# A top-32 mask moved from VectorE to ScalarE and GpSimd in a fused attention and mixture-of-experts kernel

## The chip, the core and the metric

The kernel runs on one core of one Trainium2 chip. The metric is the device time of one execution in microseconds (us). The core's engines work side by side, each through its own queue in order, and wait for each other through semaphores: PE (TensorE: matmuls and transposes, with PEld for its weight loads), DVE (VectorE), ACT (ScalarE), POOL (GpSimd) and SP (SyncE, which here only issues DMAs). Line numbers (L270) are those of the kernel before.

## The reference, cut to what matters

```python
# q, k, v: (8, 8, 576, 64) float32; top_k = 32
scores = scale * np.matmul(q, k.transpose(0, 1, 3, 2))
kth = np.partition(scores, -top_k, axis=-1)[..., -top_k:-top_k + 1]
scores = np.where(scores >= kth, scores, -1000000000.0)
attn = np.exp(scores - np.max(scores, axis=-1, keepdims=True))
attn = attn / (np.sum(attn, axis=-1, keepdims=True) + 1e-09)
x = np.matmul(attn, v)               # rearranged to (4608, 512)
# mixture of experts, 8 experts, each token to the one with the largest logit
logits = x @ w_gate
...
h = np.maximum(x_sorted[lo:hi] @ w1[e], 0.0)   # w1[e]: 512 x 1024
y_sorted[lo:hi] = h @ w2[e]                    # w2[e]: 1024 x 512
```

Every row of scores keeps its 32 largest entries; the others get weight zero. The weighted values then go, token by token, through one of eight two-layer networks.

## The kernel before, in words

**Tiling.** There are 8 batches. A batch has 4 units, and a unit is a pair of heads, 576 x 576 scores each. The rows of a unit are cut into 9 tiles of 128 rows by 576 columns, and the tiles into 5 groups: four pairs (one tile of each head) and one single tile (the last 64 rows of both heads). A *step* is one group. A batch has 20 steps, the kernel 160 steps and 288 tiles.

**A step.** `scores` (L202) multiplies q by k on PE (L212) and ACT copies the result from PSUM to the tile `s` in SBUF (L217). `weights` (L220) does the top 32 on DVE. First the 576 columns are *folded*: `hl` holds the larger and the smaller of column j and column j + 288 (L233, L234, two-input instructions). On the larger half, four rounds of MAX8 (L241, the eight largest) and three of MATCH_REPLACE8 (L251, which strikes them out) give its 32 largest; one more MAX8 (L248) looks at the smaller half. From both lists come the threshold `thr` (L261, L265) and, on POOL, a small value `over` (L266) that tells at the end whether the fold could have missed something; then an exact version below L609 would run, which it doesn't here. While the rounds go on, ACT makes minus the row's maximum (`nbias`, L243) and the exponential of all 576 scores (`w`, L245). At the end of the step DVE multiplies `w` by the mask "score at least threshold" and sums the rows in the same instruction, with the sum read out after it (L270). `transposed` (L276) turns `w` around on PE (L284, L292), and ACT copies it out (L287, L289, L295, L297). After the single tile of a unit, `outputs` (L299) multiplies by v (L314), and transposes the result to px and pl (L318 to L323). Its inner function `scaled` (L328 to L351) divides by the row sums on DVE: L336 reads px.

**Batches and experts.** After a batch's last unit, `route` (L355) finds each token's expert, and five scatters on POOL (L395) write the tokens to rows in DRAM sorted by expert. Each full block of 128 tokens of one expert is then a block of work for `block` (L477): PE transposes (L481), two layers of matmuls (L491, L500), ACT between (L483, L496, L504, which makes `y`), and a scatter to the output on POOL (L505). Its inputs, 4 MB of weights among them, are loaded through SP (`load_block`, L462). A block is cut into 17 pieces, which the main loop hands out from the sixth step of a batch on (L594 to L596). Batches 2 to 7 have blocks to do beside attention; the blocks that come out of the last batch run alone, after all attention: this is the *tail*.

**What sets the order.** The main loop (L577) writes, for step i: the scores of step i + 1, the weights of step i, `settle` (the scaling of a finished unit, and `route`), `close` (transposes and outputs) of step i - 1, and pieces of expert blocks. A scheduler then puts each engine's queue in order: it follows the written order where it can and fills in later instructions where it expects a gap. The buffers of the pools bound how far it can run ahead: `s` and `hl` have 2, `w` has 3.

Of the kernel before, what the change touches and what calls it, by code (L numbers as in the profile page):

```python
# [9 lines left out]
F32 = mybir.dt.float32  # L10
I32 = mybir.dt.int32
AF = mybir.ActivationFunctionType
# [4 lines left out]

TOP_K = 32
NEG = -3.0e38
BIG = 3.0e38  # L20
EPS = 1e-9

# [19 lines left out]
def kernel(  # L42
# [139 lines left out]
    def load_unit(b, u):  # L182
        n = SimpleNamespace(u=u)
        qkb = k.load.tile([P, 2, S], F32, name="qkb")
        nc.sync.dma_start(qkb, qk[b, u, :, :, :])
        n.q, n.k = qkb[:, 0, :], qkb[:, 1, :]
        n.v = k.load.tile([P, KC, P], F32, name="vb")
        nc.sync.dma_start(n.v, v[b, u, :, :].rearrange("(c p) d -> p c d", p=P))
        return n
# [12 lines left out]
    def scores(n, tiles):  # L202
        todo = []
        got = []
        for i in tiles:
            ps = k.ps_s.tile([P, 2, SM], F32, name="sc")
            todo += [(ps, h, rows, cols) for h, rows, cols in parts(i)]
            got.append(ps)
        for j in range(2):
            for ps, h, rows, cols in todo:  # L210
                d = slice(h * D, (h + 1) * D)
                nc.tensor.matmul(  # L212
                    ps[rows, j, 0:HF], n.q[d, cols], n.k[d, j * HF:(j + 1) * HF], start=True, stop=True
                )
        s = k.att.tile([P, 2, 2, HF], F32, name="s")
        for m, ps in enumerate(got):
            nc.scalar.copy(s[:, m, :, :], ps[:, :, 0:HF])  # L217
        return s

    def weights(n, tiles, s):  # L220
        m_all = range(len(tiles))
        m2 = slice(0, len(tiles))
        tops = tops_of[k.top % NTOP]
        k.top += 1
        nbias = k.small.tile([P, 2], F32, name="nbias", bufs=3)
        w = k.att.tile([P, 2, S], F32, name="w", bufs=3)
        flat = [s[:, m, :, :].rearrange("p j k -> p (j k)") for m in m_all]
        if k.exact:
            src = list(flat)
            width = S  # L230
        else:
            hl = k.att.tile([P, 2, 2, HF], F32, name="hl")
            nc.vector.tensor_tensor(hl[:, 0, m2, :], s[:, m2, 0, :], s[:, m2, 1, :], op=ALU.max)  # L233
            nc.vector.tensor_tensor(hl[:, 1, m2, :], s[:, m2, 0, :], s[:, m2, 1, :], op=ALU.min)  # L234
            src = [hl[:, 0, m, :] for m in m_all]
            width = HF
        scr = k.att.tile([P, 2, width], F32, name="scr")
        R = TOP_K // 8
        for r in range(R):
            for m in m_all:  # L240
                nc.vector.max(out=tops[:, m, r * 8:(r + 1) * 8], in_=src[m])  # L241
            if r == 0:
                nc.scalar.mul(nbias[:, m2], tops[:, m2, 0], -scale)  # L243
                for m in m_all:
                    nc.scalar.activation(w[:, m, :], flat[m], AF.Exp, scale=scale, bias=nbias[:, m:m + 1])  # L245
                if not k.exact:
                    for m in m_all:
                        nc.vector.max(out=tops[:, m, TOP_K + 1:TOP_K + 9], in_=hl[:, 1, m, :])  # L248
            if r < R - 1:
                for m in m_all:  # L250
                    nc.vector.match_replace(  # L251
                        out=scr[:, m, :], in_to_replace=tops[:, m, r * 8:(r + 1) * 8],
                        in_values=src[m], imm_value=NEG,
                    )
                    src[m] = scr[:, m, :]
        c = 2 * tiles[0] if len(tiles) == 2 else 2 * NC
        if k.exact:
            thr = tops[:, :, TOP_K - 1]
        else:
            both = k.small.tile([P, 2, 9], F32, name="both")  # L260
            nc.vector.tensor_tensor(  # L261
                both[:, m2, :], _back(tops[:, m2, TOP_K - 9:TOP_K]), tops[:, m2, TOP_K:TOP_K + 9], op=ALU.min
            )
            thr = k.small.tile([P, 2], F32, name="thr", bufs=3)
            nc.vector.tensor_reduce(thr[:, m2], both[:, m2, :], axis=AX.X, op=ALU.max)  # L265
            nc.gpsimd.tensor_tensor(  # L266
                n.over[:, c:c + len(tiles)], tops[:, m2, TOP_K + 8], thr[:, m2], op=ALU.subtract
            )
        for m in m_all:
            nc.vector.scalar_tensor_tensor(  # L270
                out=w[:, m, :], in0=flat[m], scalar=thr[:, m:m + 1], in1=w[:, m, :],
                op0=ALU.is_ge, op1=ALU.mult, accum_out=n.z[:, c + m:c + m + 1],
            )
        return w

    def transposed(n, tiles, w):  # L276
        pair = len(tiles) == 2
# [236 lines left out]

    with ExitStack() as st:
        open_pools(st, False)
        unit_of = {(0, 0): load_unit(0, 0)}

        work = [(b, u, g) for b in range(B) for u in range(U) for g in groups]
        per_batch = U * len(groups)  # L520
# [23 lines left out]
        def close(last):  # L544
            nonlocal late
            b, u, g, w = last
            n = unit_of[b, u]
            transposed(n, g, w)
            if g == groups[-1]:
                late = (b, u, outputs(n))  # L550

        def settle():
            nonlocal late, left
# [18 lines left out]
                left += new * PIECES  # L572
                ahead()

        s_next = scores(unit_of[0, 0], groups[0])
        last = None
        for i, (b, u, g) in enumerate(work):  # L577
            n = unit_of[b, u]
            if g == groups[0]:
                open_unit(n)  # L580
                b2, u2 = (b, u + 1) if u + 1 < U else (b + 1, 0)
                if b2 < B:
                    unit_of[b2, u2] = load_unit(b2, u2)
            s_now = s_next
            if i + 1 < len(work):
                b2, u2, g2 = work[i + 1]
                s_next = scores(unit_of[b2, u2], g2)
            w = weights(n, g, s_now)
            settle()
            if last is not None:  # L590
                close(last)
            last = (b, u, g, w)
            at = i % per_batch
            if at >= FIRST:  # L594
                rest = left - (KEEP if b == B - 1 else 0)
                pieces(-(-rest // (per_batch - at)))  # L596
# [13 lines left out]
    with tc.If(again > 0):  # L610
        with ExitStack() as st:
# [7 lines left out]
            with tc.For_i(0, B, 1) as b:  # L619
                x = k.xp.tile([P, KC, XW], F32, name="x")  # L620
                nc.vector.tensor_copy(x[:, :, Dm + 1].bitcast(I32), ids)
                lg = k.small.tile([P, KC, E], F32, name="lg")
                for u in range(U):
                    n = load_unit(b, u)
                    open_unit(n)
                    for g in groups:
                        transposed(n, g, weights(n, g, scores(n, g)))
                    outputs(n)(x, lg)
                route(x, lg)
                nc.vector.tensor_scalar_add(ids, ids, S)  # L630
# [52 lines left out]
```

## Time and profile before

| | |
|---|---|
| median of 7 runs | 1796.81 us (1793.19 to 1799.84) |
| profiled execution | 1794.58 us, span 1792.9 us |
| mean granted clock of PE | 0.853 |
| busy: DVE, ACT, POOL | 1416.6, 721.3, 120.1 us |
| last threshold found | 1440.6 us |
| period of a unit on DVE, batches 0 and 1 | 43.3 us |

Times inside the span count from its start. A row of a group gives the line, the engine, the operation, the tiles it writes and reads, the shape and the count; then its busy time in us and the mean duration of one in ns; then how long the engine stood idle just before it and who ended that. A row of the timeline gives start and length in us, and in brackets the idle time before it with its releaser. Instructions on one engine can overlap at their ends, so the distance between two starts is what one takes from the engine's time. The granted clock is TensorE's, as a share of full speed.

The period of a unit and the time of the last threshold were read from the starts of L266, which runs once a step when the threshold is there: in batches 0 and 1 the five steps of a unit lie 8.6, 11.4, 8.5, 7.7 and 7.0 us apart.

### The profile page before, as it was taken

Reading aid. Unit: us, or ns where it says so; the run is one execution under the profiler, and the core shown is the slowest. Engines: PE = TensorE matmul, PEld = TensorE weight load, DVE = VectorE, ACT = ScalarE, POOL = GpSimd, SP = SyncE. Lnnn points to the kernel's source line nnn. Section 1 sums busy time; section 2 is a strip of 40 time slices with the busy share of each in tenths; the row PEclk is TensorE's granted clock in tenths of the full one; section 3 lists DMA queues with packets and bytes.
Section 4 is the critical chain, followed back from the end, with each engine's and each line's share of the span. In section 5 each row is a group of like instructions: output and inputs, shape, how many; then the busy total and the mean of one; then the engine's idle time right before and its main releaser. Section 6 shows DMA issues by size and latency. Waiting matters only on the chain. (4 is left out here: it accounts for less than half of the span.)

```text
span 1792.9 us, 24778 instructions
## 1 busy us (share of the span) xinstructions
PE 1537.1 (86%) x8126; PEld 982.7 (55%) x8126; DVE 1416.6 (79%) x4967; ACT 721.3 (40%) x1429; POOL 120.1 (7%) x268
## 2 busy tenths in 40 slices
PE   5777777879887999799979997999799938999996
PEld 3344444446444765476646654756466616666664
DVE  8999999999999999999999999999999930000000
ACT  3444444444444444454545553545454411111111
POOL 0000100010001000100010001000100010000000
PEclk9866666669866999699979996999799868999999
DMA  1000100034002640255326502653254138888883
GB/s 55 21 21 21 48 21 21 21 107 167 27 21 101 232 168 33 90 214 203 127 74 231 202 33 80 235 188 130 67 221 151 61 97 316 295 304 301 299 299 143
DMA packets 107561, 244.00 MB, mean 136 GB/s; under 512 B 5535, under 2 KB 26015, under 8 KB 107425
## 3 DMA queue, kind: packets, MB, share of 16 engines
q1 hardware_dynamic: 101040, 223.43, 34.6%
q0 software_dynamic: 6384, 18.92, 2.9%
q8 instruction: 66, 1.08, 0.2%
q14 instruction: 71, 0.57, 0.1%
HBM read 221.05 MB, written 23.11 MB: 136 GB/s over the span
## 5 line engine op out<-in xcount | busy, mean ns | idle before, releaser
L212 PE MATMUL sc<-qkb 64*128 64x288 f32 (+1 forms) x1280 | 377.4, 540 | 45.0 <-ACT s L217 38.5
L491 PE MATMUL ph<-xTs,w 128*128 128x128 f32 x2752 | 345.1, 283 | 28.6 <-ACT xTs L483 23.8
L241 DVE MAX8 tops<-scr 128x8 f32<-128x288 f32 x864 | 356.7, 448 | 1.2
L491 PEld LDWEIGHTS ph<-xTs,w 128*128 128x128 f32 x2752 | 327.9, 197 | 52.5 <-ACT xTs L483 34.4
L500 PE MATMUL py<-w,hT 128*128 128x512 f32 x688 | 316.9, 600 | 0.0
L284 PE MATMUL wTm<-ident,w 128*128 128x128 f32 x1152 | 218.7, 340 | 105.1 <-DVE w L270 83.6
L284 PEld LDWEIGHTS wTm<-ident,w 128*128 128x128 f32 x1152 | 168.1, 175 | 178.4 <-ACT nbias L243 44.5
L212 PEld LDWEIGHTS sc<-qkb 64*128 64x128 f32 (+1 forms) x1280 | 175.3, 217 | 163.5 <-ACT s L217 69.1
L251 DVE MATCH_REPLACE8 scr<-tops,scr 128x288 f32<-128x288 f32 x576 | 251.3, 443 | 0.0
L217 ACT COPY s<-sc 128x576 f32<-128x576 f32 x288 | 174.4, 641 | 181.0 <-DVE w L270 98.4
L270 DVE SCALAR_TENSOR_TENSOR w<-s,thr,w 128x576 f32<-128x576 f32 x288 | 224.1, 810 | 1.5 <-ACT w L245 0.3
L245 ACT ACTIVATE w<-s,nbias 128x576 f32<-128x576 f32 x288 | 212.4, 772 | 4.3
L500 PEld LDWEIGHTS py<-w,hT 128*128 128x128 f32 x688 | 124.0, 192 | 126.3 <-issue 126.0
L287 ACT COPY wT<-wTm 128x512 f32<-128x512 f32 x256 | 144.1, 590 | 97.9 <-PE wTm L284 97.1
L314 PE MATMUL po<-wT,vb 128*64 128x288 f32 x1024 | 154.9, 450 | 1.2 <-ACT wT L289 1.2
L496 ACT ACTIVATE hT<-ph 128x512 f32<-128x512 f32 x86 | 51.4, 598 | 206.4 <-PE ph L491 206.1
L241 DVE MAX8 tops<-hl 128x8 f32<-128x288 f32 x288 | 127.8, 451 | 0.0
L251 DVE MATCH_REPLACE8 scr<-tops,hl 128x288 f32<-128x288 f32 x288 | 125.9, 443 | 0.0
L233 DVE TENSOR_TENSOR hl<-s 128x576 f32<-128x576 f32 (+1 forms) x160 | 109.9, 687 | 19.7 <-ACT s L217 19.6
L248 DVE MAX8 tops<-hl 128x8 f32<-128x288 f32 x288 | 120.2, 446 | 0.0
L314 PEld LDWEIGHTS po<-wT,vb 128*64 128x64 f32 x1024 | 74.1, 150 | 80.0 <-issue 37.9
L234 DVE TENSOR_TENSOR hl<-s 128x576 f32<-128x576 f32 (+1 forms) x160 | 110.3, 690 | 0.0
(113 smaller groups left out, 938.9 us busy)
## 6 DMA issues: line engine op xcount, KB each, us to landing
w<-in_moe_w_dram SPq DMA_DIRECT2D x86, 2048.0 KB, 12.7
qkb<-in_qk_dram SPq DMA_DIRECT2D x32, 576.0 KB, 3.8
xg<-x_rows SPq DMA_DIRECT2D x43, 257.0 KB, 2.7
vb<-in_v_dram SPq DMA_DIRECT2D x32, 320.0 KB, 3.2
x_rows<-blank SPq DMA_DIRECT2D x9, 257.0 KB, 4.9
out_dram<-y,xg POOLq DMA_INDIRECT x43
x_rows<-x,posi POOLq DMA_INDIRECT x40
wg<-in_moe_w_gate_dram SPq DMA_DIRECT2D x1, 16.0 KB
```

The lines of the kernel that those rows point to most:

```text
L212: nc.tensor.matmul(ps[rows, j, 0:HF], n.q[d, cols], n.k[d, j * HF:(j + 1) * HF], start=True, stop=True)
L217: nc.scalar.copy(s[:, m, :, :], ps[:, :, 0:HF])
L241: nc.vector.max(out=tops[:, m, r * 8:(r + 1) * 8], in_=src[m])
L245: nc.scalar.activation(w[:, m, :], flat[m], AF.Exp, scale=scale, bias=nbias[:, m:m + 1])
L248: nc.vector.max(out=tops[:, m, TOP_K + 1:TOP_K + 9], in_=hl[:, 1, m, :])
L251: nc.vector.match_replace(out=scr[:, m, :], in_to_replace=tops[:, m, r * 8:(r + 1) * 8], in_values=src[m], imm_value=NEG,)
L270: nc.vector.scalar_tensor_tensor(out=w[:, m, :], in0=flat[m], scalar=thr[:, m:m + 1], in1=w[:, m, :], op0=ALU.is_ge, op1=ALU.mult, accum_o ...
L284: nc.tensor.transpose(pm[:, c * P:(c + 1) * P], w[:, m, c * P:(c + 1) * P], ident)
L287: nc.scalar.copy(n.wT[:, :, m, tiles[0] * P:(tiles[0] + 1) * P], pm4)
L314: nc.tensor.matmul(po[r, 0:HF], lhsT, rhs, start=(c == 0), stop=(c == KC - 1))
L491: nc.tensor.matmul(ph[:, f, :], n.w1[:, 0, dt, fc * P:(fc + 1) * P], xT[:, dt, :], start=(dt == 0), stop=(dt == DT - 1),)
L500: nc.tensor.matmul(py, hT[:, f, :], n.w2[:, 0, f, :], start=(f == 0), stop=(f == FT - 1))
```

## The change

`weights` is taken apart into four functions.

- `fold` makes `hl`. It is called for step i + 1 within the search of step i, ahead of its fourth round.
- `search` runs the rounds and makes `thr`. `nbias` is now made on POOL, and so is a new small value `low`, the threshold times 2^120.
- `depths` has ACT compute Relu(2^120 x (thr - s)) for each of the 288 tiles, into `w`: zero where the score is kept, a huge number elsewhere.
- The new `weights` subtracts it from the score on POOL (a two-input instruction over 128 x 576, one for each tile), and then ACT takes the exponential, now summing the rows itself. Masked entries become exp of a hugely negative number, zero.

The masked multiplication on DVE (L270) is gone. Exponential and Relu now both come after the threshold. `s` has three buffers where it had two; scores are written two steps ahead where it was one. The inputs of two units are loaded at the start, and a unit's inputs are asked for after the outputs of the unit two before it, where it was at the start of the unit before it. In the step, `settle` and `close` now stand between the search and `depths`.

```diff
-        s = k.att.tile([P, 2, 2, HF], F32, name="s")
+        s = k.att.tile([P, 2, 2, HF], F32, name="s", bufs=2 if k.exact else 3)
...
+    def fold(tiles, s):
+
+        m2 = slice(0, len(tiles))
+        hl = k.att.tile([P, 2, 2, HF], F32, name="hl")
+        nc.vector.tensor_tensor(hl[:, 0, m2, :], s[:, m2, 0, :], s[:, m2, 1, :], op=ALU.max)
+        nc.vector.tensor_tensor(hl[:, 1, m2, :], s[:, m2, 0, :], s[:, m2, 1, :], op=ALU.min)
+        return hl
...
         for r in range(R):
+            if r == R - 1:
+                between()
             for m in m_all:
                 nc.vector.max(out=tops[:, m, r * 8:(r + 1) * 8], in_=src[m])
             if r == 0:
-                nc.scalar.mul(nbias[:, m2], tops[:, m2, 0], -scale)
-                for m in m_all:
-                    nc.scalar.activation(w[:, m, :], flat[m], AF.Exp, scale=scale, bias=nbias[:, m:m + 1])
+                nc.gpsimd.tensor_scalar_mul(nbias[:, m2], tops[:, m2, 0], -scale)
...
+        low = k.small.tile([P, 2], F32, name="low", bufs=3)
+        nc.gpsimd.tensor_scalar_mul(low[:, m2], thr[:, m2], STEEP)
...
-        for m in m_all:
-            nc.vector.scalar_tensor_tensor(
-                out=w[:, m, :], in0=flat[m], scalar=thr[:, m:m + 1], in1=w[:, m, :],
-                op0=ALU.is_ge, op1=ALU.mult, accum_out=n.z[:, c + m:c + m + 1],
-            )
+        return low, nbias
+
+    def depths(tiles, s, low):
+
+        w = k.att.tile([P, 2, S], F32, name="w", bufs=3)
+        for m in range(len(tiles)):
+            nc.scalar.activation(
+                w[:, m, :], s[:, m, :, :].rearrange("p j k -> p (j k)"), AF.Relu,
+                scale=-STEEP, bias=low[:, m:m + 1],
+            )
         return w
+
+    def weights(n, tiles, s, w, nbias):
+
+        c = 2 * tiles[0] if len(tiles) == 2 else 2 * NC
+        for m in range(len(tiles)):
+            nc.gpsimd.tensor_tensor(
+                w[:, m, :], s[:, m, :, :].rearrange("p j k -> p (j k)"), w[:, m, :], op=ALU.subtract
+            )
+            nc.scalar.activation(
+                w[:, m, :], w[:, m, :], AF.Exp, scale=scale, bias=nbias[:, m:m + 1],
+                accum_out=n.z[:, c + m:c + m + 1],
+            )
...
-        unit_of = {(0, 0): load_unit(0, 0)}
+        unit_of = {(0, u): load_unit(0, u) for u in range(2)}
...
                 late = (b, u, outputs(n))
+                b2, u2 = divmod(b * U + u + 2, U)
+                if b2 < B:
+                    unit_of[b2, u2] = load_unit(b2, u2)
...
-            s_now = s_next
-            if i + 1 < len(work):
-                b2, u2, g2 = work[i + 1]
-                s_next = scores(unit_of[b2, u2], g2)
-            w = weights(n, g, s_now)
+
+            def between():
+                if i + 1 < len(work):
+                    hl_of[i + 1] = fold(work[i + 1][2], s_of[i + 1])
+
+            low, nbias = search(n, g, s_of[i], hl_of.pop(i), between)
             settle()
             if last is not None:
                 close(last)
+            w = depths(g, s_of[i], low)
+            if i + 2 < len(work):
+                s_of[i + 2] = ready(i + 2)
+            weights(n, g, s_of.pop(i), w, nbias)
             last = (b, u, g, w)
```

## The prediction, on record before the result

> **What bounds the kernel now.** I read the engine shares of the page, then the stages, then the order of instructions inside one group of rows.
>
> ```profile
> PE   1537.1 (86%) x8126; PEld 982.7 (55%) x8126; DVE 1416.6 (79%) x4967; ACT 721.3 (40%) x1429; POOL 120.1 (7%) x268
> ```
>
> Over the span PE looks busiest, but that is a mean over two unlike parts. The stages (columns: length, then busy time of PE, PEld, DVE, ACT, POOL with counts, granted clock, DMA share, GB/s) tell them apart:
>
> ```profile
> 60.00:190.00 130.00, 98.77 (x422) 53.79 (x420) 129.56 (x438) 58.40 (x117) 2.82 (x15) 0.69 0.07 22
> 414.00:546.00 132.00, 113.33 (x532) 67.31 (x532) 129.33 (x438) 61.42 (x122) 5.37 (x17) 0.78 0.12 42
> 594.00:726.00 132.00, 126.44 (x700) 81.69 (x700) 128.99 (x436) 64.95 (x130) 6.71 (x18) 0.91 0.32 114
> 774.00:908.00 134.00, 130.25 (x798) 85.71 (x796) 131.42 (x440) 68.67 (x135) 8.07 (x21) 0.99 0.42 149
> 956.00:1086.00 130.00, 122.89 (x702) 79.09 (x702) 129.27 (x437) 64.96 (x130) 7.29 (x19) 0.96 0.32 115
> 1134.00:1267.00 133.00, 127.71 (x786) 83.97 (x784) 130.48 (x436) 67.99 (x134) 7.69 (x19) 1.00 0.41 149
> 1315.00:1441.00 126.00, 120.47 (x674) 77.46 (x669) 120.86 (x410) 60.78 (x122) 7.40 (x19) 0.96 0.30 109
> 1485.00:1793.00 308.00, 280.68 (x1592) 202.46 (x1591) 0.00 (x0) 44.29 (x75) 18.70 (x19) 0.98 0.75 277
> ```
>
> These are the last fifteen steps of batches 0, 2, 3, 4, 5, 6 and 7, and the tail. Up to 1441 us DVE is busy without a break: it sets the pace. But PE, which does expert blocks beside attention from batch 2 on, comes close: in batches 4 and 6 it is 97% busy at a clock of 0.99 to 1.00, so it has nothing left there. The tail holds no attention; the change doesn't reach it. What DVE does:
>
> ```profile
> L270 DVE SCALAR_TENSOR_TENSOR w<-s,thr,w 128x576 f32<-128x576 f32 x288 | 224.1, 810 | 1.5 <-ACT w L245 0.3
> L245 ACT ACTIVATE w<-s,nbias 128x576 f32<-128x576 f32 x288 | 212.4, 772 | 4.3
> ```
>
> ```profile
> 18.71 0.80 DVE L270 SCALAR_TENSOR_TENSOR w<-s,thr,w 128x576 f32<-128x576 f32 x1
> 19.44 0.08 DVE L270 DVE_READ_ACCUMULATOR w<-s,thr,w 128x1 f32 x1
> 19.44 0.81 DVE L270 SCALAR_TENSOR_TENSOR w<-s,thr,w 128x576 f32<-128x576 f32 x1
> 20.18 0.08 DVE L270 DVE_READ_ACCUMULATOR w<-s,thr,w 128x1 f32 x1
> ```
>
> One lasts 0.81 us, but the next starts 0.735 us after it: that is what one takes from DVE's time.
>
> **The change, part by part.** *The mask leaves DVE:* 288 x 0.735 = 212 us, 36 x 0.735 = 26.5 us a batch. How much of it reaches the end is a matter of the stage. Batches 0 and 1 are DVE's alone (PE 98.8 of 130 at clock 0.69): 2 x 26.5 = 53. In the later six batches the first five steps (48 us, PE about 38.5) are DVE's too: 9 x 0.735 = 6.6 each, 40 in all. For their last fifteen steps (27 instructions, 19.8 us) I take as PE's floor its busy time times the clock, over 0.98: 113.3 x 0.78 / 0.98 = 90 for batch 2, so all 19.8 comes; 117 for batch 3 (132 - 117 = 15), 132 for batch 4 (2), 120 for batch 5 (10), 130 for batch 6 (3), 118 for batch 7 (8). Together 53 + 40 + 20 + 38 = **151 us**. When DVE's stall goes, PE is late next.
>
> *Relu on ACT:* 288 of the shape of L245, 0.77 us: 222 us, on an engine with 58 to 69 us of work in 130. Off the path as occupancy. The sum that moves from DVE to the exponential's accumulator may add an instruction on ACT; DVE's kind takes 0.08 us, so 0 to 23 us more, hidden in the same idle time. Relu, Exp and Copy already alternate behind one table load.
>
> *The subtraction on POOL:* 288 of 128x576 with two inputs. No row has that. Below: a memset of 128x513 at 517 ns, so 0.58 us. Above: the affine select of 128x128, 282 ns, as it stands is 2.2 ns an element, 1.27 us, doubled for two inputs 2.54. Taking off a fixed 129 ns (the 128x8 iota) leaves 1.2 ns an element: 0.8 us for one input, 1.5 for two; I take **1.5 us**, nearest to that row. So 288 x 1.5 = 432 us of about 1300, plus small ones (low, over, nbias at 0.19 us): no bound by occupancy.
>
> The Trainium skill (GPSIMD Engine Reference, Elementwise side by side) measured 4497 ns for a two-input add of 2048 elements; as an estimate that is 1.26 us for 576, and the sum would keep its size.
>
> *A longer way from threshold to weights.* Before, the masked weights stand 1.2 us after the threshold. Now: low 0.2, Relu 0.77, subtraction 1.5, exponential 0.77, some 0.3 for hand-overs: 3.5 us, 2.3 later. Most is covered, as PE takes the weights one step later. The cover is thin at one place, once a unit: DVE scales a unit's output (L336) after two more searches, and needs px from PE:
>
> ```profile
> 285.33 1.19 PE L323 MATMUL pl<-wg,oT 128*128 128x16 f32 x10
> ...
> 289.59 0.69 DVE L336 TENSOR_TENSOR x<-px,rz 128x512 f32<-128x512 f32 x1
> ```
>
> px ends at 285.39 here, so 4.2 us to spare. The change brings L336 forward by five masks (3.7 us) and px back by 2.3: 6.0 are needed. Over the 32 units the spare time is 3.7 to 5.1 us in batches 0 and 1, 4.4 to 7.8 in batch 2, mostly 5 to 8 later: new stalls of about 1.6 us in each of 8 units, 3 us in batch 2, 3 in first units later: **19 us**. Where PE is the floor the stall costs nothing more. Its bounds: 0 (PE's clock rises) to 2.5 times that with 2.54 us a subtraction.
>
> *Folds against subtractions.* The trace cannot show whether DVE's two-input folds (L233, L234, 0.67 us each) and POOL's reads get in each other's way; its POOL instructions are too small. Bounds: 0, and one subtraction a step (1.5 us x 160 = 240 us). The subtractions of a pair should end about 5 us after its threshold; the fold after next starts about 4.7 after it (a new step of 7.2 us, less 2.5): they just touch. I take 0.3 us a step where DVE is the pace, 85 steps: **26 us**.
>
> The Trainium skill (SBUF — State Buffer, Who interferes with whom) speaks against this change: a DVE instruction with two SBUF inputs and a GpSimd one that reads SBUF shut each other out, and whichever comes second waits to the end of the other. By it the term would grow towards its upper end if the two drift into step, and be 0 if folds always come first.
>
> *POOL's queue.* low, nbias and the subtraction stand behind the scatter L505, which waits for ACT's y:
>
> ```profile
> 796.10 1.01 POOL L505 DMA_INDIRECT out_dram<-y,xg  x1 [13.20 <-ACT y L504]
> 797.14 0.20 POOL L266 TENSOR_TENSOR over<-tops,thr 128x2 f32<-128x2 f32 x1
> ```
>
> The instruction behind it was ready at 794.0 and ran at 797.1. So far nobody waits for it; now ACT's Relu does, and behind that ACT's evacuations and PE. y, scatter and low are 0.69 + 1.01 + 0.2 = 1.9 us; for 24 blocks 0 to 46 us; I take 0.5 each, **12 us**. The five route scatters of a batch stand there too, where PE has time.
>
> *Folds and scores further ahead, and the load:* 0. The trace already has the next pair's fold (16.85) ahead of the present threshold (18.27), and a unit's inputs land in 3.8 us, a unit (43 us) before their use; with SP's longest wait, 37 us, that still holds. At worst a late load costs its landing, 8 x 3.8 = 30 us. A gain from a third s buffer is bounded by DVE's waits for s, 19.6 us. *At the end:* the last weights come 2.3 us later, in full: **2 us**.
>
> Sum: 151 - 19 - 26 - 12 - 2 = 92. The profiled execution took 1794.6 us (span 1792.9), so 1703; the median of the runs is 2.2 us above it: **1705 us**.
>
> **Rivals.** *A, full relief:* no losses, 1797 - 149 = 1648; with PE's floor softer than its busy share too, 1797 - 210 = 1587. For it: DVE idles under 1% in the first stage. Against: the spare time at L336. *B, slower:* POOL holds DVE. If one subtraction takes near 2.5 us, POOL is busy 5.6 of a step's 7.3 us, and each of the two folds meets one in flight and waits on average half of it: 2.5 us a pair against 1.47 gained, about 1.0 x 128 + 0.5 x 32 = 144 lost in place of the gain; minus what PE's floor hides (half), 1797 + 72 = **1870**. It decides from 1.47 us lost per pair, one whole subtraction. For it: only the bounds above. Against: the select's row gives 1.5. *C, moved, not removed:* ACT, held by Relus that wait for POOL, makes PE late wherever PE is the floor, and each step keeps its old pitch: 1755 to 1797, say 1780.
>
> **How the numbers follow.** Forecast (1650 to 1755) 0.58, A 0.13, B 0.20, C 0.09. The range 1630 to 1840 leaves out the lower part of A (0.05) and the upper of B (0.10); forecast and A alone would be 1587 to 1755. Faster by over 0.2%: 0.58 + 0.13 + 0.06 of C = 0.77; within 0.2%, about what this kernel's runs can tell from no change, 0.03; slower 0.20.
>
> **What would show it.** Right: in batches 0 and 1 a unit's period falls from 43.3 us to about 39, in batches 4 and 6 the fifteen steps stay near 131; DVE's idle time names px; POOL's subtraction reads near 1.5 us; L233 and L234 lengthen only now and then. Wrong: folds at 1.5 us and more (B), ACT's Relu waiting long for low while PE idles in batches 4 and 6 (C), or no idle time on DVE at all (A).

## The result and the profile after

The changed kernel took 1806.5 us (median; 1799.5 to 1813.7) beside 1797.0 us for the kernel before: ratio 1.0054, 95% interval 1.0044 to 1.0064. It is slower by half a per cent where 5% faster was forecast. Lines below are those of the changed kernel (L293); the profiled execution has a span of 1803.3 us.

What was to leave DVE did leave it. The page's engine shares, to be set beside those of before:

```profile
PE 1506.3 (84%) x8126; PEld 967.6 (54%) x8126; DVE 1283.2 (71%) x4391; ACT 915.2 (51%) x1845; POOL 624.7 (35%) x876
```

DVE is busy 133 us less, and POOL 505 us more. But the whole did not become shorter, so DVE must now stand idle. The stages say where (last fifteen steps of batches 0, 2, 4 and 6; columns as in the prediction):

```profile
55.00:176.00 121.00, 86.74 (x422) 49.36 (x420) 118.18 (x384) 76.27 (x156) 51.17 (x72) 0.74 0.08 23
389.50:512.00 122.50, 106.02 (x590) 65.70 (x589) 119.42 (x384) 81.50 (x169) 52.32 (x76) 0.89 0.15 52
737.70:881.00 143.30, 135.66 (x797) 88.71 (x794) 117.03 (x386) 84.86 (x170) 55.09 (x77) 0.98 0.38 137
1121.30:1269.80 148.50, 141.58 (x820) 92.99 (x821) 118.00 (x387) 86.05 (x173) 56.19 (x76) 0.96 0.37 132
```

Batches 0 and 2 got shorter (121 and 122.5 us, before 130 and 132) and DVE is still busy there nearly all the time: 118 us for 384 instructions, where 130 us less 27 masks of 0.735 us would be 110. Batches 4 and 6 got *longer* (143 and 148.5, before 134 and 133), and there DVE is idle for 26 and 30 us. PE is busy longer as well: 135.7 and 141.6 us, before 130.3 and 127.7; in batch 6 a part of that is more work in the stretch (820 instructions, before 786). So there are two kinds of loss: DVE needs more time for what it does, and DVE stands idle. The lengths of the batches, from the first threshold of one to the first of the next (the eighth to its last threshold), give the balance:

```
batch              0      1      2      3      4      5      6      7    then
before         171.6  175.7  179.9  180.5  181.5  178.1  181.5  173.3   352.4
after          157.0  167.4  168.3  178.5  190.6  191.8  197.2  173.3   360.2
difference     -14.6   -8.3  -11.6   -2.0   +9.1  +13.7  +15.7    0.0    +7.8
```

Thirty-six us are won by batch 3 and lost again by batch 6; the end adds 8. The last two columns belong together: of the 43 expert blocks (64 matmuls of the first layer each), 20 are now done after the last threshold, before 19, so batch 7 has one less. The tail, which the prediction held to be out of the change's reach, was reached in this way.

**First loss, on DVE itself.** The groups of the two folds before, then, after the change, of the subtraction, of the two folds, and of ACT's read-out of its accumulator:

```profile
L233 DVE TENSOR_TENSOR hl<-s 128x576 f32<-128x576 f32 (+1 forms) x160 | 109.9, 687 | 19.7 <-ACT s L217 19.6
L234 DVE TENSOR_TENSOR hl<-s 128x576 f32<-128x576 f32 (+1 forms) x160 | 110.3, 690 | 0.0
```

```profile
L293 POOL TENSOR_TENSOR w<-s,w 128x576 f32<-128x576 f32 x288 | 430.7, 1512 | 287.7 <-ACT w L283 286.1 <-DVE thr L269 0.7
L225 DVE TENSOR_TENSOR hl<-s 128x576 f32<-128x576 f32 (+1 forms) x160 | 133.4, 833 | 54.0 <-ACT s L218 53.0
L226 DVE TENSOR_TENSOR hl<-s 128x576 f32<-128x576 f32 (+1 forms) x160 | 125.9, 787 | 0.0
L296 ACT ACTIVATION_READ_ACCUMULATOR w<-w,nbias 128x1 f32 x288 | 54.4, 189 | 0.0
```

The folds took 687 and 690 ns in the mean before; now 833 and 787, together 39 us more. The 39 us lie on 43 of the 320 folds, some 0.9 us each, four to seven of them in every batch, and each of the 43 started while a subtraction was running. The timeline of batch 0 shows how one grows (start, length):

```profile
122.43 0.75 DVE L225 TENSOR_TENSOR hl<-s 128x576 f32<-128x576 f32 x1
123.35 3.28 POOL L293 TENSOR_TENSOR w<-s,w 128x576 f32<-128x576 f32 x2
123.47 1.90 DVE L226 TENSOR_TENSOR hl<-s 128x576 f32<-128x576 f32 x1
...
145.81 2.77 POOL L293 TENSOR_TENSOR w<-s,w 128x576 f32<-128x576 f32 x2 [1.65 <-ACT w L283]
146.36 0.91 DVE L373 TENSOR_TENSOR lg<-lg,lt 128x40 f32<-128x40 f32 x1
147.57 1.07 DVE L374 TENSOR_TENSOR lg<-lg,lt 128x40 f32<-128x40 f32 x1
```

The fold at 122.43 runs ahead of the subtractions and takes 0.75 us. Its twin starts 0.12 us after a subtraction has begun and takes 1.90. L373 and L374 add 40 elements to a row, 0.19 us each before; here they last 0.91 and 1.07 us, each ending with one of the two subtractions. So it is with the DVE instructions with two inputs in SBUF that meet a subtraction: folds +39.1 us, `both` (L265) +10.5, `doubt` (L355) +7.4, the sums of `lg` +13.2: **70 us**, where the prediction had 26. Others beside a subtraction don't show it: L361, which has one input in PSUM, took 693 ns in the seven cases that met one and 692 otherwise, and MAX8, which has one input, 445 and 444.

**Second loss, waiting for the weights.** One pair of tiles in batch 0, from the threshold to the transposes:

```profile
114.87 0.15 DVE L269 TENSOR_REDUCE thr<-both 128x2 f32<-128x18 f32 x1
115.54 1.44 ACT L283 ACTIVATE w<-s,low 128x576 f32<-128x576 f32 x2 [3.63 <-POOL low L271]
116.39 2.78 POOL L293 TENSOR_TENSOR w<-s,w 128x576 f32<-128x576 f32 x2 [0.73 <-ACT w L283]
117.83 0.78 ACT L296 ACTIVATE w<-w,nbias 128x576 f32<-128x576 f32 x1 [0.85 <-POOL w L293]
118.75 1.12 PE L309 MATMUL wTm<-ident,w 128*128 128x128 f32 x4 [6.30 <-ACT w L296]
119.20 0.78 ACT L296 ACTIVATE w<-w,nbias 128x576 f32<-128x576 f32 x1 [0.50 <-POOL w L293]
```

From 115.02 to 119.98 it is 5.0 us to the second tile, and that is one of the shortest: over the 128 pairs the median is 6.4 us and the mean 7.0 (before, the second mask was done 1.8 us after the threshold, the first 1.1). The prediction's 3.5 us is the time of the first tile alone. ACT stands still 0.85 and 0.50 us for POOL, and PE 6.3 us for ACT. In all PE stands idle 176.5 us before L309 for these exponentials; before, it was 83.6 us for the masks. What DVE waits for most is `px`; before, and after (the us in all, how many, the longest):

```profile
DVE x L336 <- PE px L318: 7.3, 1, 7.3
```

```profile
DVE x L361 <- PE px L343: 84.1, 29, 8.8
```

Of the 84.1, batch 0 and then batch 6 have:

```profile
DVE x L361 <- PE px L343: 1.4, 3, 0.5
```

```profile
DVE x L361 <- PE px L343: 16.8, 4, 5.8
```

So the wait stands where PE is near its floor, not in the batches where the prediction had put it. (Not all of it is a loss by the change: run 3 below has 54.7 us of it left.) One of batch 4 in the timeline:

```profile
787.13 0.78 ACT L296 ACTIVATE w<-w,nbias 128x576 f32<-128x576 f32 x1 [0.57 <-POOL w L293]
...
788.50 0.77 ACT L296 ACTIVATE w<-w,nbias 128x576 f32<-128x576 f32 x1 [0.49 <-POOL w L293]
789.27 0.38 ACT L340 COPY oT<-po 128x288 f32<-128x288 f32 x1
...
790.39 2.15 PE L348 MATMUL pl<-wg,oT 128*128 128x16 f32 x10
790.43 0.69 DVE L361 TENSOR_TENSOR x<-px,rz 128x512 f32<-128x512 f32 x1 [6.00 <-PE px L343]
```

PE had finished its second product at 787.4, but ACT copied it out only at 789.27: two exponentials that wait for POOL stood ahead of that copy in ACT's queue. That is 1.85 us of the 6.00 that DVE waits here. PE idles, and afterwards is slow (ten small matmuls in 2.15 us; 1.19 in the prediction's line of before). Over the whole of batches 4, 5 and 6 PE's idle time grew from 13, 16 and 14 us to 24, 25 and 23, and its busy time went from 168, 162 and 167 to 166, 167 and 174: the larger part is idle time.

After the gap of 6.30 us above, L309's four transposes took 1.12 us, and 0.66 us where the gap was 0.49. The page TensorE: Matmul & The Clock Gate of the Trainium skill (Why this matters for your kernels) says that idle gaps of more than about 3 us put the array back to half its clock. The trace agrees as far as it goes: after each of the 14 gaps of over 5 us the four took 1.11 or 1.12 us. But after 18 gaps of 1 to 2 us they took 1.11 in the median too, so the gap just before does not decide alone.

### The profile page after: what moved, and what is told of

Same layout as the page of the kernel before. It is cut to its first block, busy times and chain, and to the rows that moved or that the text cites. A ratio compares the mean times of both kernels' runs of the same rounds, so it can differ in the third digit from the quotient of the medians.

```text
span 1803.3 us, 25580 instructions
## 1 busy us (share of the span) xinstructions
PE 1506.3 (84%) x8126; PEld 967.6 (54%) x8126; DVE 1283.2 (71%) x4391; ACT 915.2 (51%) x1845; POOL 624.7 (35%) x876
## 5 line engine op out<-in xcount | busy, mean ns | idle before, releaser
L293 POOL TENSOR_TENSOR w<-s,w 128x576 f32<-128x576 f32 x288 | 430.7, 1512 | 287.7 <-ACT w L283 286.1
L309 PE MATMUL wTm<-ident,w 128*128 128x128 f32 x1152 | 212.0, 326 | 181.2 <-ACT w L296 176.5
L213 PE MATMUL sc<-qkb 64*128 64x288 f32 (+1 forms) x1280 | 344.2, 528 | 17.6 <-ACT s L218 10.7
L296 ACT ACTIVATE w<-w,nbias 128x576 f32<-128x576 f32 x288 | 223.4, 776 | 181.7 <-POOL w L293 180.6
L309 PEld LDWEIGHTS wTm<-ident,w 128*128 128x128 f32 x1152 | 156.4, 166 | 258.2 <-ACT w L296 227.0
L283 ACT ACTIVATE w<-s,low 128x576 f32<-128x576 f32 x288 | 212.8, 774 | 119.1 <-POOL low L271 111.3
L213 PEld LDWEIGHTS sc<-qkb 64*128 64x128 f32 (+1 forms) x1280 | 166.7, 215 | 114.1 <-issue 43.7
L225 DVE TENSOR_TENSOR hl<-s 128x576 f32<-128x576 f32 (+1 forms) x160 | 133.4, 833 | 54.0 <-ACT s L218 53.0
L530 POOL DMA_INDIRECT out_dram<-y,xg x43 | 43.6, 1014 | 335.8 <-ACT y L529 330.8
L250 POOL TENSOR_SCALAR nbias<-tops 128x2 f32<-128x2 f32 (+1 forms) x160 | 35.1, 220 | 306.5 <-DVE thr L269 180.2
L226 DVE TENSOR_TENSOR hl<-s 128x576 f32<-128x576 f32 (+1 forms) x160 | 125.9, 787 | 0.0
```

What stands on the lines that cost most here:

```text
L213: nc.tensor.matmul(ps[rows, j, 0:HF], n.q[d, cols], n.k[d, j * HF:(j + 1) * HF], start=True, stop=True)
L283: nc.scalar.activation(w[:, m, :], s[:, m, :, :].rearrange("p j k -> p (j k)"), AF.Relu, scale=-STEEP, bias=low[:, m:m + 1],)
L293: nc.gpsimd.tensor_tensor(w[:, m, :], s[:, m, :, :].rearrange("p j k -> p (j k)"), w[:, m, :], op=ALU.subtract)
L296: nc.scalar.activation(w[:, m, :], w[:, m, :], AF.Exp, scale=scale, bias=nbias[:, m:m + 1], accum_out=n.z[:, c + m:c + m + 1],)
L309: nc.tensor.transpose(pm[:, c * P:(c + 1) * P], w[:, m, c * P:(c + 1) * P], ident)
```

## The experiments

Two theories, and a rival to both. *Port*: DVE's two-input instructions and POOL's reads shut each other out, which costs some 70 us. *Late weights*: the longer way from the threshold makes `px`, and PE, late. *Rival*: the new order (scores and folds ahead, loads later) is what costs. Each run was timed beside the kernel before; differences between runs are those of the ratios, times 1797 us. In runs 1 to 3 the weights have other values, so the result is not that of the reference, but the work is the same: PE has 8126 matmuls in each.

**1. POOL writes but does not read.** The subtraction is replaced by two memsets per tile that take as long together; for that the tiles `w` are 796 wide. (Each experiment's profile has its own line numbers, a few off.)

```diff
-            nc.gpsimd.tensor_tensor(
-                w[:, m, :], s[:, m, :, :].rearrange("p j k -> p (j k)"), w[:, m, :], op=ALU.subtract
-            )
+            for _ in range(2):
+                nc.gpsimd.memset(w[:, m, :], 0.0)
```

> The subtraction is replaced by two POOL memsets of 796 elements (about 0.7 us each by the 513-element row, together near the 1.41 us of the subtraction): POOL only writes, and the way from threshold to weights keeps its length. The weights are then a constant instead of the masked exponential. Theory 'late weights' (the way from threshold to weights grew from 1.6 to 5 us, so DVE waits for px and PE waits for weights and cools): the folds go back to 220 us of busy time (they are 259 in the changed kernel), DVE's wait for px stays near 80 us, the time is about 1765 us. Theory 'port' (the subtraction and DVE's two-input instructions shut each other out, 70 us of DVE time): 1730 us or less. Theory 'order' (the new written order alone costs the time): about 1800 us.

1738.4 us, ratio 0.9665 (0.9638 to 0.9693): 70 us less than the changed kernel, between the two ranges and nearer to that of *port*. The groups:

```profile
L295 POOL MEMSET w<- 128x796 f32 x576 | 418.0, 762 | 321.1 <-ACT w L284 317.8
L226 DVE TENSOR_TENSOR hl<-s 128x576 f32<-128x576 f32 (+1 forms) x160 | 110.0, 687 | 49.1 <-ACT s L219 49.0
L227 DVE TENSOR_TENSOR hl<-s 128x576 f32<-128x576 f32 (+1 forms) x160 | 109.9, 687 | 0.0
```

POOL is as busy as before (418 us), in the same places, and the folds are back at 687 ns. POOL's subtraction, which reads SBUF, holds DVE; a memset, which only writes, doesn't. The way to the weights is as long as it was (median 6.6 us), and the wait for `px` grew to 108 us: part of the time that DVE gets back it spends there. That the time fell by the same 70 us by which the instructions had been longer is chance, since the waits changed too.

The Trainium skill says this in SBUF — State Buffer, under Who interferes with whom: a DVE instruction with two SBUF inputs contends with a GpSimd instruction that reads SBUF, not with one that only writes it. These two runs agree on both halves, with 833 and 687 ns.

**2. Weights early, POOL still reads.** The exponential runs during the search, unmasked, and feeds PE; Relu and subtraction still run after the threshold, into a tile `d` that nobody reads.

```diff
+                w = k.att.tile([P, 2, S], F32, name="w", bufs=3)
+                for m in m_all:
+                    nc.scalar.activation(
+                        w[:, m, :], s[:, m, :, :].rearrange("p j k -> p (j k)"), AF.Exp, scale=scale,
+                        bias=nbias[:, m:m + 1], accum_out=n.z[:, c + m:c + m + 1],
+                    )
...
-            w = depths(g, s_of[i], low)
+            d = depths(g, s_of[i], low)
...
-            weights(n, g, s_of.pop(i), w, nbias)
+            weights(n, g, s_of.pop(i), d, None)
```

> The exponential is taken from the unmasked scores as soon as the row maximum is known, and PE gets that; Relu and subtraction still run, 288 each, into a tile that nobody reads. The mask is left out of the result. Late weights: DVE's wait for px (84 us) and PE's for weights vanish, POOL's subtractions still lengthen the folds: 1670 to 1700 us. Port: folds and small two-input instructions keep some 70 us of extra time and the kernel stays above 1780. Order: stays at 1800.

1758.5 us, ratio 0.9777 (0.9751 to 0.9804): 50 us less than the changed kernel, above the 1670 to 1700 of *late weights* and below the 1780 of *port*. Folds still 133.8 and 123.7 us. PE's wait before the transposes falls from 176.5 to 60.7 us, but DVE's wait for `px` only from 84.1 to 52.7; it was expected to vanish. So neither theory is the whole loss.

**3. Both at once:** run 2 with the memsets of run 1 in place of the subtraction.

> Both together: early unmasked weights, and memsets for the subtractions. Late weights and port as the two causes: the full relief, 1630 to 1660 us, PE being the limit in batches 3 to 7. Order: 1780 or more.

1663.4 us, ratio 0.9248 (0.9223 to 0.9273), 3 us above the expected range: 145 us less than the changed kernel, where the two alone give 70 and 50. Each loss hides part of the other: DVE that is held by POOL would otherwise wait for `px`, and the other way round. A unit takes 36.3 us in batches 0 and 1 (43.3 before). This is what the change would bring without either loss. The same batch lengths as above, from the profiles, say where each run gives time back against the changed kernel (us):

```
                      batches 0 to 2   3 to 7   then
run 1 (no reading)              15.5     54.0   -1.7
run 2 (weights early)            3.9     33.6    9.4
run 3 (both)                    47.6     86.9    7.1
```

Neither loss belongs to one stage. Even the port costs most where PE is near its floor. And in batches 0 to 2 late weights cost little only as long as the port hides them: in run 1 DVE waits 31 us for `px` there (7 in the changed kernel), and batch 0 gains next to nothing (156.6 us, 157.0). What DVE waits in batches 3 to 7 is not all loss either. Its idle time there is 142 us in the changed kernel and still 95 in run 3, with this wait for `px`:

```profile
DVE x L365 <- PE px L347: 54.7, 13, 8.1
```

There PE, busy 91 to 95% of each of these batches, is near its floor, and DVE waits for it.

**4. The order alone.** The order of the changed kernel, the mask on DVE as before, the exponential early.

```diff
+        for m in m_all:
+            nc.vector.scalar_tensor_tensor(
+                out=w[:, m, :], in0=s[:, m, :, :].rearrange("p j k -> p (j k)"), scalar=thr[:, m:m + 1],
+                in1=w[:, m, :], op0=ALU.is_ge, op1=ALU.mult, accum_out=n.z[:, c + m:c + m + 1],
+            )
-        return low, nbias
+        return w
...
-            w = depths(g, s_of[i], low)
...
-            weights(n, g, s_of.pop(i), w, nbias)
```

> The changed kernel's order (folds one step ahead, scores two ahead, three s buffers, loads after the outputs), but the mask back on DVE with the early exponential, and nbias on ACT. Late weights or port: within 1% of the kernel before, 1785 to 1805 us. Order: 1806 us or more, and the wait for px or the slow second step of batches 5 and 7 (26 us) appear here too.

1785.0 us, ratio 0.9931 (0.9905 to 0.9958). The rival falls: with the mask on DVE the order brings 12 us, it costs none. Its batches: 170.5, 175.0, 180.3, 177.7, 181.7, 176.3, 181.9, 167.2 us. From here the balance of the whole change reads: order -12, mask off DVE -123 (run 3 against run 4), its two losses +145, sum +10.

**5. Folds ahead of the first round, scores three steps ahead.** The folds should be done before the subtractions begin.

```diff
-            if r == R - 1:
+            if r == 0:
                 between()
...
-            if i + 2 < len(work):
-                s_of[i + 2] = ready(i + 2)
+            if i + 3 < len(work):
+                s_of[i + 3] = ready(i + 3)
...
-        s = k.att.tile([P, 2, 2, HF], F32, name="s", bufs=2 if k.exact else 3)
+        s = k.att.tile([P, 2, 2, HF], F32, name="s", bufs=2 if k.exact else 4)
```

> The changed kernel with one thing moved: the fold of the next step is called ahead of the first round of a search, not the fourth, and scores are written three steps ahead (four s buffers), so that DVE's folds run around the threshold, before POOL's subtractions of that step begin about 1.2 us after it. The work is the same. Port theory (the loss is in folds that meet subtractions in flight): folds back to 0.69 to 0.75 us each, 45 to 65 us less DVE time, and as in the run without POOL's reads the wait for px then grows to about 105 us, so 1740 to 1765 us. Rival (a subtraction costs DVE its time wherever the folds stand, or the time is only that of the late weights): folds stay at 0.8 us, 1790 to 1810 us.

1778.5 us, ratio 0.9897 (0.9864 to 0.9931), between the two ranges. The folds fell to 123.9 and 121.3 us, 25 us above before in place of 39: the place matters, but 40 of the folds still meet a subtraction, now mostly that of one step earlier. Two things were changed, so run 11 takes them apart.

**6. The new mask only where DVE sets the pace,** in batches 0 to 2; from batch 3 on the mask on DVE. `own` names the tiles that are masked on DVE; they have the early exponential, the others go the new way.

```diff
+            own = range(len(g)) if b >= 3 else ()
-            low, nbias = search(n, g, s_of[i], hl_of.pop(i), between)
+            low, nbias, w = search(n, g, s_of[i], hl_of.pop(i), between, own)
```

> The order of the changed kernel everywhere; the mask by Relu, POOL and late exponential only in batches 0, 1 and 2, the mask on DVE with the early exponential from batch 3 on. Theory (the gain is real where DVE alone is the pace, and late weights cost where PE is near its floor): batches 0 to 2 as in the changed kernel (157, 167, 168 us), batches 3 to 7 as in the run with only the order (177 to 182): 1785 less 13, 8 and 8 gives 1750 to 1765 us. Rival (what is won early comes back as waiting for expert blocks or at the end): 1780 to 1800 us.

1756.2 us, ratio 0.9764 (0.9726 to 0.9803), inside the expected range. Batches 0 to 2 take 157.1, 166.0 and 174.9 us (batch 2 is 6.6 us longer than in the changed kernel), the others 176.9, 181.7, 176.2, 181.7 and 166.7, as in run 4. What is won early stays won; against the mask on DVE the new mask gains in batches 0 to 2 and loses in batches 3 to 7.

**7. One tile of each pair.** The first tile of a pair on DVE, the second by POOL (144 of 288).

```diff
+            own = (0,) if len(g) == 2 or u % 2 else ()
```

> The changed kernel, but of each pair of tiles the first is masked on DVE with the early exponential, and only the second by Relu, POOL's subtraction and the late exponential (single tiles alternate): 144 of 288 tiles each way. Theory (lock and late weights both grow with the number of tiles in the chain): half of DVE's 212 us leave, the folds' lock halves to 25 to 40 us, the way from threshold to weights is some 3.5 us instead of 5.0 and the wait for px falls below 40 us: 1735 to 1775 us. Rival (one subtraction a step is enough for the lock, and one late tile for the late weights): 1785 to 1815 us.

1806.8 us, ratio 1.0050 (1.0029 to 1.0071). The time is in the rival's range, 32 us above the theory's. Batches 0 to 2 keep 24 of the 34 us that the changed kernel wins there, but batches 3 to 7 take 924 us, the changed kernel's 931, run 4's 885. The wait for `px` did fall below 40 us, as the theory had it, and that for `s` from 53.0 to 37.2. But DVE is busy 70 us more than in the changed kernel, and it has a new wait, for ACT's early exponentials:

```profile
DVE hl L225 <- ACT s L218: 37.2, 24, 5.4
DVE x L379 <- PE px L361: 33.9, 13, 10.8
DVE w L288 <- ACT w L256: 19.6, 9, 3.6
```

**8. `low` and `nbias` on DVE,** out of POOL's queue.

```diff
-                nc.gpsimd.tensor_scalar_mul(nbias[:, m2], tops[:, m2, 0], -scale)
+                nc.vector.tensor_scalar_mul(nbias[:, m2], tops[:, m2, 0], -scale)
...
-        nc.gpsimd.tensor_scalar_mul(low[:, m2], thr[:, m2], STEEP)
+        nc.vector.tensor_scalar_mul(low[:, m2], thr[:, m2], STEEP)
```

> The changed kernel with low and nbias made on DVE, not on POOL; the subtraction stays on POOL. If the queue on POOL (low and nbias behind scatters and subtractions) were what makes the weights late: 1780 us or less. If it is a small term, as the few waits of ACT for low say (the change's 320 small instructions cost DVE 20 to 30 us where it is the pace): 1795 to 1820 us.

1825.7 us, ratio 1.0181 (1.0130 to 1.0232), a little above the range: the 320 small instructions last 85 us on DVE (359 and 173 ns each), DVE is busy 52 us more in all, and the wait for `px` fell only from 84 to 76 us. So moving the small instructions doesn't pay. It does not settle POOL's queue, since the subtraction still stands in it: in the pairs its wait after its Relu grew from 10.6 to 35.5 us. In the changed kernel `low` starts more than 0.3 us after its threshold in 23 of the 160 steps, 57.5 us in all, 33 of them behind the five route scatters, once in each of seven batches. What that costs is open.

**9. As 6, and the single tile that ends a unit on DVE in batches 0 to 2.**

```diff
+            own = range(len(g)) if b >= 3 or len(g) == 1 else ()
```

> The mixed kernel (Relu, POOL and late exponential only in batches 0 to 2), and there the single tile that ends each unit goes back to DVE with the early exponential: 96 of 288 tiles by POOL. Theory (in the stages that DVE paces, what is left of the late weights is the wait for px, and px hangs on the unit's last tile): the second step of a unit in batches 0 to 2 falls from 12.2 us to about 10 for 0.74 us more in another step, 12 units by about 1.5 us: 1735 to 1750 us. Rival (px waits as long on the pair ahead of the single tile): 1755 to 1770 us.

1756.6 us, ratio 0.9764 (0.9734 to 0.9795): no gain, and in the rival's range. The second step of a unit fell by about 1 us, less than expected, the single tile's own step grew by 0.8 (6.5 to 7.3 us), and the step after it by up to 1.3.

**10. The single tile on DVE in all batches** of the changed kernel.

```diff
+            own = (0,) if len(g) == 1 else ()
```

> The changed kernel with only the single tile that ends each unit masked on DVE with the early exponential, in all batches: 256 of 288 tiles by POOL. If px waits because the unit's last tile is late: the wait for px falls from 84 us to under 40, against 32 x 0.74 = 24 us more DVE work: 1765 to 1795 us. If px waits because PE is behind with the pairs too, above all from batch 3 on: the wait stays over 60 us and the time 1800 to 1825 us.

1770.3 us, ratio 0.9843 (0.9805 to 0.9881), 38 us less than the changed kernel. The waits for `px` fell from 29 to 14, but those that are left are long (58.0 us in all): the time is in the first range, the wait between the two. The gain is in batches 4 to 7 (187.1, 182.9, 185.8 and 158.2 us), none of it in batches 0 to 3.

**11. Scores three steps ahead, folds where they were** (the second half of the diff of run 5).

> The changed kernel with the scores three steps ahead and four s buffers, the fold left ahead of the fourth round. It takes apart the run in which both were changed (1778 us). If that gain came from the place of the folds: 1798 to 1815 us here. If it came from the scores being there earlier: 1770 to 1785 us, and the folds keep their 0.8 us.

1755.5 us, ratio 0.9760 (0.9722 to 0.9797): 53 us less than the changed kernel, with every mask still on POOL, and 15 us below even the lower range. So the gain of run 5 did not come from the folds' place. Here they keep 129.5 and 131.6 us, and run 5, which moves them too, is 25 us slower than this one, for a reason that I didn't pin down. DVE's waits in this run:

```profile
DVE x L361 <- PE px L343: 70.3, 30, 9.2
DVE hl L225 <- ACT s L218: 26.6, 18, 5.5
```

The wait for `s` halves (53.0 us in the changed kernel). All of the gain lies in batches 3 to 7: 172.2, 184.0, 176.6, 182.5 and 162.4 us; batches 0 to 2 are 5 us longer.

**12 to 14. What the third step of lead is.** Run 12 is the control: run 4 with the same lead. Run 13 has the fourth buffer and the old lead. Run 14 joins 10 and 11.

> Control for the run with scores three steps ahead: the same fourth s buffer and the same three steps in the kernel that has only the order (mask on DVE, early exponential; 1785 us with two steps ahead). Theory (the missing lead is a need that the new mask makes, since the scores stay in use until POOL has subtracted and ACT and PE meet them late): 1780 to 1788 us, no gain to speak of, for DVE waits only 13 us for s there. Rival (the third step ahead helps this program whatever masks it, as PE's blocks hold the scores up): 1745 to 1770 us.

1778.6 us, ratio 0.9889 (0.9858 to 0.9919): 8 us less than run 4, with intervals that overlap, against 53 us with the new mask. Nearly all of what the lead is worth is a need that the new mask makes.

> The changed kernel with a fourth s buffer, scores still written two steps ahead. It takes the run with three steps apart into buffer and order. If ACT's copies into s were held because the buffer is in use until POOL has subtracted: 1755 to 1775 us, and the wait for s falls from 53 us to under 30. If it is the place of the scores in the queues of PE and ACT (behind transposes and exponentials that wait for the late weights): 1798 to 1812 us.

1793.6 us, ratio 0.9989 (0.9969 to 1.0010), between the two ranges: the buffer alone brings 12 of the 53 us and cuts the wait for `s` to 34 us. The larger part comes with the third step in the written order. That scores then stand ahead of transposes that wait for late weights is the likely reason; no run takes it apart further.

> Both repairs in the changed kernel: scores three steps ahead with four s buffers (1755 us alone, won in batches 3 to 7), and the single tile that ends each unit masked on DVE with the early exponential (1770 us alone, through the wait for px). If the two waits are separate they add: 1806 less 51 and 36 gives 1715 to 1735 us. If they are one wait seen at two places, or the lock and PE's floor take over: 1745 to 1760 us.

1770.9 us, ratio 0.9843 (0.9815 to 0.9871). The two repairs don't add; together they are 15 us slower than run 11 alone. Against run 11 DVE waits 26 us less for `px`, but it is busy 23 us more, and its mask waits 22.7 us for early exponentials; `both` loses 19.5 us to the subtractions (46.9 us in all, 27.4 before). The time lies above both ranges: that they are one wait seen at two places is not shown by it.

The fastest versions that keep the mask are runs 6, 9 and 11, each 2.4% below the kernel before; runs 4, 5, 10, 12 and 14 are 0.7 to 1.6% below it.

## Why the prediction was wrong

*What DVE is relieved of, 151 us.* Measured 123 us (run 4 to run 3). By batch, in order: 27, 26, 28, 15, 2, 6, 4 and 14 us; predicted 26.5 three times, then 22, 9, 17, 10 and 15 (batch 7 of run 3, too, has one expert block less). Batches 0 to 2 were right. The miss is mostly in the first five steps of the later batches, which I took for DVE's alone: in batches 3 to 7 without either loss they still take 42 to 50 us, with a second step of 13 to 21. The floors of PE for the last fifteen steps of batches 3 to 6, predicted 117, 132, 120, 130, came out at 121, 136, 121, 136; that of batch 7 was too high (118, and 104).

*The subtraction, 1.5 us:* right; 1.41 us is the median and 1.51 the mean. POOL is no bound by occupancy (35% busy), and rival B's 2.5 us did not come true. *Accumulator read-out, 0 to 23 us on ACT:* 54 us, outside; what it cost in time no run shows.

*Folds against subtractions, 26 us: this step failed in size.* It was 70 us. The mechanism was there, its bounds (0 to 240) held it, and the folds did lengthen only now and then. But I counted only the folds, and only the 85 steps where DVE is the pace. The folds lost 39 us, in every batch; and I missed the small instructions with two inputs (`both`, `doubt`, `lg`), which lost 31 us, up to 1.2 us each. In the last two units of batch 0 the second step takes 12.2 us in place of the 9.6 of run 3, and 1.6 of that are the sums of `lg`, none the folds. By the profiles, taking POOL's reads away gave back 54 of 68 us in batches 3 to 7, where I had counted 25 of the 85 steps.

*Late weights, 19 us for `px` and 12 for POOL's queue: this step failed in its place.* The way is 6.4 us (median) and at best 4.8, not 3.5: two tiles go through POOL in turn, and I had counted one. Then I looked for the stalls where DVE has little spare time to `px`, batches 0 to 2, and wrote "Where PE is the floor the stall costs nothing more." The runs showed the opposite: weights that are early again give back 34 us in batches 3 to 7 and 9 after them, and 4 in batches 0 to 2. PE at 97% has no room to be late: it idles before the transposes, and ACT's copies stand behind exponentials that wait for POOL. The stalls that I had forecast for batches 0 to 2 do appear, 31 us of them, once POOL no longer holds DVE (run 1); in the changed kernel the port hides them. The whole of it is 50 us while POOL holds DVE, 75 when it doesn't (run 1 against run 3). What POOL's queue costs no run shows; `low` stood 57.5 us in it, more than half behind the route scatters, which I had put at nothing.

*Folds and scores ahead, 0.* Alone it is -12 us; but one step more, with one more buffer, was worth 53 us once the weights were late. I bounded the gain by DVE's waits for `s` in the old trace (19.6 us), which the change itself raised to 53.

*The sum* treated the losses as separate and small: 59 us. They are 145, and not separate: 70 and 50 when taken away alone. Rival C, each step at its old pitch because ACT and PE are late at PE's floor, comes nearest for batches 3 to 7, which even grew from 895 to 931 us; it had 9%. Rival A's price for full relief, 1648, is close to run 3's 1663.

What stays open: why the folds' earlier place costs time in run 5, and how the 75 us of late weights divide between ACT's queue, PE's waiting and PE's slower running. Each edit is also scheduled anew, so the order elsewhere can change with it; how much of the 15 to 25 us between runs 5, 11 and 14 is of that kind no run shows. An earlier copy of `oT` past the waiting exponentials was not tried.

## What to carry to other kernels

Before two-input work goes to POOL, list *every* DVE instruction with two inputs in SBUF, the tiny ones too: here each could lose up to 1.2 us to a POOL instruction of 1.4, and memsets that only write cost them nothing. Where an engine is 97% busy, don't take later inputs to be hidden by its backlog: here they cost 34 us in the batches where PE was near its floor, and a longer lead for the work that feeds it (one step and one buffer) brought back 53. A change with a gain in one stage and a loss in another is worth applying by stage: the same order with the new mask in batches 0 to 2 alone is 2.4% faster than before, with it in all batches 0.5% slower.

## What the runs showed of the hardware that I had not expected

An addition of 128x40 on DVE, 0.19 us alone, took 0.91 and 1.07 us beside POOL's subtractions. The wait does not shrink with the instruction that waits: the longest `both` (128x18 or 128x9 elements, 0.17 us in the mean before) took 1.39 us, the longest fold (0.75 before) 1.96. 576 memsets of 128x796 (762 ns each) at the same place left the folds at 687 ns. ACT's accumulator costs a separate read-out of 189 ns, more than twice that of DVE (82 ns in the mean).
